# A planner's lengths of transfers, the place of one weight's sums, and the rank of early norms, in a fused attention and expert kernel

## The chip, the cores and the metric

The kernel runs on one core of one Trainium2 chip. The metric is the time of one execution in device microseconds, as the median of several runs. The core has a matrix engine (TensorE, PE in the profile), a vector engine (VectorE, DVE), a scalar engine (ScalarE, ACT), GpSimd (POOL), and SyncE (SP), which here only issues transfers. Each of them works through its own list of instructions in order.

## The reference, cut to what matters

Eight sequences of 576 tokens with 8 heads of 64 go through a linear attention without softmax, are normed, and become 4608 rows of 512. Each row goes to the one of eight experts with the largest logit, up to a capacity, in the order of the rows, and the expert is two matrix products with a Relu between them.

```python
kv = np.einsum('bhsd,bhse->bhde', k, v)
out = np.einsum('bhsd,bhde->bhse', q, kv)
rms = np.sqrt(np.mean(out * out, axis=-1, keepdims=True) + 1e-06)
x = (out / rms * g_norm) ...            # to [4608, 512]
logits = x @ w_gate
expert_idx = np.argmax(logits, axis=1)
...
h = np.maximum(np.einsum('ecd,edf->ecf', disp, w1), 0.0)
y = np.einsum('ecf,efd->ecd', h, w2)
out[i] = gate_w[i] * y[expert_idx[i], pos[i]]
```

## The kernel before, in words

**Attention, batch by batch.** For each of the eight batches (b0 to b7) `load` brings k, v and q in halves through SyncE's queue. `kv_products` multiplies k by v (L740), copies the result off the accumulators (`kvs`), turns it (L764) and forms the gate's products (L773). `unit` then makes the five blocks of the output (L801), each half copied to `o_sb` (L698 on ScalarE, L700 on VectorE), and `squares` squares them on ScalarE (L822) and sums them on VectorE (L827). `route` turns the sums into the row scale (L851, L855, L858, L865 to L870), forms the logits (`lt`, `lg`), their maximum (L899) and the one-hot choice `ohe` (L919). TensorE counts positions (the products at L944, "place" below, which wait for `ohe`), and enters the tokens into a table in PSUM (L984). The batch's rows then go to `x_dram` through GpSimd's queue (L1003, L1005).

**The early expert.** After b2 one expert is picked. Its weights come through the buffer `raw` in quarters of 512 KB each (L346): first w1, and then, through the same buffer, w2. Each weight is split into two half-precision parts. `split_weight` takes a bound on its size for each of eight pieces, either by VectorE's maximum (`top`, L362) or by ScalarE's sum of absolute values (`sum`, L366). `most` and `spread` (L370 to L377, one product on TensorE) and `scale` (L381 to L386) make a factor of it, then ScalarE writes eight upper halves (`w1h`, L391) and VectorE eight lower halves (`w1l`, L397). After b4 the table is read a first time, and the first 384 rows of the early expert are gathered (L448, GpSimd), normed (`xm`, L456, VectorE), turned (L467, TensorE), copied (the cast at L698) and split (L475). With these TensorE forms the early products: the hidden layer (L552, evicted as `hh` by ScalarE, L557, and `hl` by VectorE, L560), and the second product (L599) of three tiles.

**The rest.** When all eight batches are in the table it is read again (L1066), the experts are ranked, and round r0 gathers the early expert's other rows (L448). Rounds r1 to r7 take the other experts in order of size, each with weights and rows of its own that are prepared beside the round before. TensorE has work almost without a gap there.

**What sets the order.** Nothing runs by priority on the chip. `Plan.place` makes the lists ahead of time: each step is an `op` with a cost for each engine that may do it, the steps that it depends on, and a key. At each turn the engine that can begin first takes, of its ready steps, the one with the smallest key. A step of kind D is a transfer; its cost is how long the planner thinks it lasts. `FREE` says when each engine begins, `WKEYS` the keys of the early weights (29.5 and 38.0 with 0.3 a step), `LOW` the key of the early rows' steps (36.5), `TOPS` which engine takes the eight bounds, `WAFTER` behind which load of k, v or q a quarter of the weight may be issued.

```python
at = max(free[e], o.at[e])
...
mine.append((at, o.at[e] - o.ahead if e in FIFO else o.key, o.n, o, t))
...
loads[-1].late = 7 if r > 1 else LATE[3]
```

Of the kernel before, what the change touches and what calls it, by code (L numbers as in the profile page):

```python
# [19 lines left out]
EARLY = 384  # L20
# [13 lines left out]
ORDER = (("k", 0), ("v", 0), ("k", 1), ("v", 1), ("q", 0), ("q", 1))  # L34
FREE = {"T": 2.0, "A": 2.5, "V": 3.0, "P": 8.0, "D": 4.5, "S": 0.7}
FIFO = ("D",)
WAIT = {}
ISSUE = (0.8, 1.6)
AHEAD = 8.0
WAFTER = ((34, 36, 38, 40), (40, 40, 40, 40))  # L40
LAG = {("T", "T"): 0.0, ("A", "T"): 0.27, ("A", "V"): 0.15, ("V", "P"): 0.16, ("V", "A"): 0.15, ("A", "A"): 0.14,
# [3 lines left out]
SQUARES = 'AAAAA'  # L45
TOPS = ('VVVV', 'AAAA')
TOKENS = ('V', 0.31)
# [13 lines left out]
LOW = 36.5  # L61
LOAD = 1.46
WKEYS = ((29.5, 0.3), (38.0, 0.3))
# [98 lines left out]
def attention_moe_kernel(  # L162
# [561 lines left out]
    def kv_products(b, ts):  # L724
# [7 lines left out]
        def product(i):  # L732
            def go(e):
                a.t = a.t or bank("a")
                for c in range(C):
                    for g in range(2):
                        h = 2 * (i % 2) + g
                        k0 = c * MD + (h * D if c < C - 1 else g * D)
                        v0 = TD + k0 if c < C - 1 else (CD + h * D, g * D)[i % 2]
                        nc.tensor.matmul(a.t[rows[g], i * D:(i + 1) * D], lhsT=kh.t[:, k0:k0 + D], rhs=vh.t[:, v0:v0 + D],  # L740
                                         start=(c == 0), stop=(c == C - 1))

            kh, vh = ts["k", i // 2][0], ts["v", i // 2][0]
            return op(("T", 0.8), go, [ts["k", i // 2][1], ts["v", i // 2][1]], key, (a,), (kh, vh))

# [44 lines left out]
    def unit(b, n, ts, kv, ready, oh):  # L790
        c, key = CHUNKS[n], b * C + n
        o_sb, done = oh.t, []
        for half in range(2):
# [12 lines left out]

            o = op(("T", 0.55), product, [qd] + ready, key + half * 0.1, (ph,), (qh, kv))
            done.append(op([("A", 0.29), ("V", 0.37)], out_, [o], key + half * 0.1, (oh,), (ph,)))
# [30 lines left out]
    def route(b, oh, ssh, outs, sums):  # L839
# [106 lines left out]

        bp = op(("T", 0.7), place, [ohe] + accs[-2:-1] + reads[-1:], FIRST)

# [42 lines left out]
        o2 = V(0.4, low_hot, [lo], takes=(lh,))  # L991
        ent = op(("T", 0.21), enter, [o, o2] + enters[-1:] + readers.pop("tab", []), FIRST, (), (rh, lh))
        enters.append(ent)
# [16 lines left out]
        for first in range(2):  # L1010
            o = op(("P", 0.6), write(first), [gate, kept], key, (), (oh,))
            ws.append(op(("D", (2.05, 1.65)[first]), None, [o], key, (), (oh,)))
            ws[-1].ahead = AHEAD
# [58 lines left out]
    def early_weights():  # L1072
# [11 lines left out]
        for i, key in ((0, W1_KEY), (1, W2_KEY)):  # L1084
            loads = [op(("S", 0.43), lambda e, i=i, p=p: load_weight(i, early["reg"], raw1, p, 4),
                        [reg] + free[p], key) for p in range(4)]
            waits.append((loads, WAFTER[i]))
            loads = [op(("D", 1.46), None, [o]) for o in loads]
            for o in loads:
# [24 lines left out]
    def early_slots():  # L1114
        key = (EARLY_AFTER + 1) * C
        early["count"] = count(cnt_early, key)
        o = op(("V", 1.0), lambda e: read_table(), enters[-1:], key)
        readers.setdefault("tab", []).append(o)

        def cut(e):  # L1120
            early["gi"], early["si"] = slots(ep, first_i[0:1, 1:2])

        o = op(("V", 0.6), cut, [o] + early["picked"], key)
        early["slots"] = [o]
        x, _, _, early["turns"] = rows(lambda: (early["gi"], None), 0, EARLY, (EARLY_AFTER + 1) * S, early["slots"], key, LOW, ep,
                                       at, lambda: bank("x"))
        early["x"] = lambda: x["rows"]
# [357 lines left out]
    def weights(r, key, after):  # L1485

        ws, sets, zs, holds = wsets[r % 2], [], [], []
        for i in range(2):
# [9 lines left out]
            for p in range(4):  # L1498
# [3 lines left out]
                regs.setdefault("op", o)  # L1502
                loads.append(op(("D", 1.46), None, [o], key, (), (raws[p],)))
                loads[-1].late = 7 if r > 1 else LATE[3]
# [188 lines left out]
```

## Time and profile before

| | us |
|---|---|
| median of 3 runs | 546.19 (542.9 to 546.37) |
| the profiled execution | 548.66 |
| its span in the trace | 546.7 |
| PE busy | 505.5 (92%) |
| DVE busy | 380.1 (70%) |
| ACT busy | 239.9 (44%) |
| POOL busy | 168.5 (31%) |

The profile is of one execution. Its span is what the trace covers, and 2.0 us lie around it. Busy shares are means over the stages; the trace shows a first stage of some 120 us, in which transfers and the routing set the pace, and then 425 us in which TensorE is nearly always busy.

### The profile page before, as it was taken

What the parts mean: (1) busy time and instruction counts of PE and PEld (TensorE: products, weight loads), DVE (VectorE), ACT (ScalarE), POOL (GpSimd) and SP (SyncE); (2) the same over time, 40 slices, a digit from 0 to 9 for tenths busy, and PEclk for the clock granted to TensorE, in tenths of its full rate; (3) what the DMA queues carried; (4) which work ended last, traced back from release to release, by engine and by line L of the source; (5) the groups of instructions that cost most, each with busy time, mean ns of one, the idle gap of its engine ahead of it and who ended that gap; (6) DMA issues with size and microseconds to landing.
All of it is one profiled execution on the core that took longest, in us unless ns stands there. A gap on an engine that the chain in (4) does not pass through costs nothing.

```text
span 546.7 us, 11248 instructions
## 1 busy us (share of the span) xinstructions
PE 505.5 (92%) x4298; PEld 345.2 (63%) x4298; DVE 380.1 (70%) x1010; ACT 239.9 (44%) x462; POOL 168.5 (31%) x174
## 2 busy tenths in 40 slices
PE   4999785759989999999999999999999999999995
PEld 4898784736446666456744764776487468648743
DVE  3499878797659899999998898397667617103800
ACT  2577463885125633826624533445262544212211
POOL 2001002000242462474327323442554164021012
PEclk9899897959999999999999999999999999999999
DMA  8999999260395885792968836463755042010010
GB/s 307 419 420 418 421 424 397 81 251 1 126 359 151 199 265 172 205 331 56 207 237 217 222 115 209 124 178 113 215 155 157 33 124 43 5 60 21 2 40 31
DMA packets 62955, 102.65 MB, mean 188 GB/s; under 512 B 38636, under 2 KB 38636, under 8 KB 61874
## 3 DMA queue, kind: packets, MB, share of 16 engines
q1 hardware_dynamic: 55296, 70.50, 40.6%
q0 software_dynamic: 7584, 31.38, 16.6%
q8 instruction: 35, 0.57, 0.4%
q14 instruction: 22, 0.18, 0.1%
q10 hardware_dynamic: 18, 0.02, 0.0%
HBM read 73.20 MB, written 20.68 MB: 172 GB/s over the span
## 4 chain that ended last, share of the span: by engine, by line
issue 32%; DVE 25%; PE 21%; POOL 13%; DMA 5%; ACT 3%; POOLq 0%; DVEq 0%; SPq 0%; ACTq 0%
DVE am L362 5%; PE yp L599 5%; POOL out_dram L629 4%; PE hp L552 4%; PE op L801 4%; PE op L552 3%; POOL pair L485 3%; DVE w1l L397 3%; POOL xm L456 3%; DVE ss L827 3%; POOL xg L448 2%; DMA xs<-pair 2%; DVE w2l L397 2%; PE a L740 2%; DVE hl L560 1%
## 5 line engine op out<-in xcount | busy, mean ns | idle before, releaser
L552 PE MATMUL hp<-xs,w1h 128*128 128x320 f16 (+6 forms) x960 | 133.9, 292 | 3.3 <-DVE hl L560 2.0
L552 PEld LDWEIGHTS <-w1h 128*128 128x128 f16 x1024 | 100.1, 98 | 39.0 <-issue 7.2
L599 PEld LDWEIGHTS <-hh 128*128 128x128 f16 x560 | 54.4, 98 | 64.2 <-issue 1.3
L629 POOL DMA_INDIRECT out_dram<-ysb,si x42 | 45.2, 1075 | 161.0 <-ACT ysb L624 154.9
L557 ACT ACTIVATE hh<-hp 128x320 f16<-128x320 f32 (+7 forms) x64 | 40.9, 639 | 101.6 <-PE hp L552 101.6
L362 DVE TENSOR_REDUCE am<-raw 128x1 f32<-128x512 f32 x120 | 75.8, 674 | 3.5 <-DMA raw<-in_moe_w_dram 3.5
L552 PE MATMUL hp<-xs,w1l 128*128 128x320 f16 (+6 forms) x480 | 72.0, 292 | 0.0
L560 DVE SCALAR_TENSOR_TENSOR hl<-hp,hh 128x320 f16<-128x320 f32 (+7 forms) x64 | 47.4, 741 | 30.2 <-ACT hh L557 29.8
L624 ACT ACTIVATE ysb<-yp,ysc 128x512 f32<-128x512 f32 (+5 forms) x41 | 28.0, 684 | 90.1 <-PE yp L599 82.7
L599 PE MATMUL yp<-w2h,hh 128*128 128x512 f16 x272 | 64.4, 379 | 0.8 <-ACT ysb L624 0.8
L599 PE MATMUL yp<-w2l,hh 128*128 128x512 f16 x272 | 64.6, 379 | 0.0
L599 PE MATMUL yp<-w2h,hl 128*128 128x512 f16 x272 | 64.3, 379 | 0.0
L552 PEld LDWEIGHTS <-w1l 128*128 128x128 f16 x512 | 50.2, 98 | 16.9 <-issue 0.5
L801 PE MATMUL op<-kv_bd,in_sb 128*128 128x144 f32 x320 | 52.3, 317 | 6.6 <-ACT o_sb L698 5.0
L397 DVE SCALAR_TENSOR_TENSOR w2l<-raw,sw,w2h 128x512 f16<-128x512 f32 x64 | 55.1, 901 | 1.8 <-ACT w2h L391 1.8
L448 POOL DMA_INDIRECT xg<-x_dram,gi x42 | 43.1, 1025 | 33.6 <-DVE gt L461 12.5
L485 POOL TENSOR_TENSOR pair<-xm,pair 128x512 f16<-128x512 f32 (+5 forms) x30 | 35.9, 1198 | 55.8 <-ACT pair L481 55.6
L801 PEld LDWEIGHTS op<-kv_bd,in_sb 128*128 128x128 f32 x320 | 46.6, 212 | 8.4 <-ACT o_sb L698 5.2
L614 DVE COPY yt<-yp 128x256 f32<-128x256 f32 (+4 forms) x7 | 2.9, 411 | 70.0 <-PE yp L608 60.8
L397 DVE SCALAR_TENSOR_TENSOR w1l<-raw,sg,w1h 128x512 f16<-128x512 f32 x64 | 50.9, 846 | 0.1
L599 PEld LDWEIGHTS <-hl 128*128 128x128 f16 x280 | 27.3, 98 | 32.5
L391 ACT ACTIVATE w2h<-raw,sw 128x512 f16<-128x512 f32 x64 | 41.5, 712 | 9.4 <-PE yp L608 7.2
(227 smaller groups left out, 574.6 us busy)
## 6 DMA issues: line engine op xcount, KB each, us to landing
raw<-in_moe_w_dram SPq DMA_DIRECT2D x64, 512.0 KB, 5.2
in_sb<-in_k_dram SPq DMA_DIRECT2D x16, 576.0 KB, 8.5
v_sb<-in_v_dram SPq DMA_DIRECT2D x32, 288.0 KB, 8.6
in_sb<-in_q_dram SPq DMA_DIRECT2D x16, 576.0 KB, 11.0
x_dram<-o_sb POOLq DMA_DIRECT2D x8, 720.0 KB, 5.4
x_dram<-o_sb POOLq DMA_DIRECT2D x8, 576.0 KB, 8.8
xg<-x_dram,gi POOLq DMA_INDIRECT x42, 4.5
out_dram<-ysb,si POOLq DMA_INDIRECT x42, 3.3
```

What stands on the lines that cost most here:

```text
L362: nc.vector.tensor_reduce(out=am()[:, p:p + 1], in_=raw[:, sl(p)], axis=AX.X, op=ALU.max, apply_absolute_value=True)
L391: nc.scalar.activation(wh[:, sl(p)], raw[:, sl(p)], AF.Copy, scale=z["s"])
L397: nc.vector.scalar_tensor_tensor(out=wl[:, sl(p)], in0=raw[:, sl(p)], scalar=z["s"], in1=wh[:, sl(p)], op0=ALU.mult, op1=ALU.subtract)
L448: nc.gpsimd.indirect_dma_start(out=self.xg[i][0:n], out_offset=None, in_=x_dram[0:self.rows, :], in_offset=bass.IndirectOffsetOnAxis(ap=se ...
L485: eng.tensor_tensor(out=pair[0:n, 1], in0=self.xm[i][0:n], in1=pair[0:n, 0], op=ALU.subtract)
L552: nc.tensor.matmul(self.view(hp)[:, v], lhsT=w[:, c, f * P:(f + 1) * P], rhs=x[:, c, u * hw:(u + 1) * hw], start=(t == 0 and c == 0), stop ...
L557: nc.scalar.activation(self.out(self.hh, j), self.view(hp), AF.Relu)
L560: nc.vector.scalar_tensor_tensor(out=self.out(self.hl, j), in0=self.view(hp), scalar=0.0, in1=self.out(self.hh, j), op0=ALU.max, op1=ALU.s ...
L599: nc.tensor.matmul(yp[0:n, 0:DM], lhsT=h[:, j, o:o + n], rhs=w[:, j, :], start=(m == 0), stop=(m == len(self.terms) - 1))
L624: nc.scalar.activation(self.ysb[0:n], yp[0:n, 0:DM], AF.Copy, scale=self.ysc[0:n, i:i + 1])
L629: nc.gpsimd.indirect_dma_start(out=(disjoint.pop() if disjoint else out)[:, :], out_offset=bass.IndirectOffsetOnAxis(ap=self.sidx[0:n, col ...
L801: nc.tensor.matmul(ph.t[:, i * 2 * XW:(i + 1) * 2 * XW], lhsT=qh.t[:, q0:q0 + P], rhs=kv.t[:, 2 * half + i].rearrange("p g x -> p (g x)"), ...
```

## The change

The planner's costs are given new values: a quarter of a weight lasts 1.27 in place of 1.46, a half of k, v or q 1.41 in place of 1.46, a batch's two writes 1.76 and 1.41 in place of 2.05 and 1.65, TensorE's products of k and v 0.68 in place of 0.8, those of the output 0.49 in place of 0.55, the place products 0.3 in place of 0.7 and the table's 0.6 in place of 0.21. The queue's start is 3.3 in place of 4.5. All four quarters of the early w1 may be issued behind the same load. The eight bounds of the early w1 become ScalarE's sums. The early rows' norms and what follows them get key 32.0 in place of 36.5.

```diff
-FREE = {"T": 2.0, "A": 2.5, "V": 3.0, "P": 8.0, "D": 4.5, "S": 0.7}
+FREE = {"T": 2.0, "A": 2.5, "V": 3.0, "P": 8.0, "D": 3.3, "S": 0.7}
...
-WAFTER = ((34, 36, 38, 40), (40, 40, 40, 40))
+WAFTER = ((34, 34, 34, 34), (40, 40, 40, 40))
...
-TOPS = ('VVVV', 'AAAA')
+TOPS = ('AAAA', 'AAAA')
...
-LOAD = 1.46
+NORM = 32.0
+LOAD = 1.41
+QUARTER = 1.27
...
-            loads = [op(("D", 1.46), None, [o]) for o in loads]
+            loads = [op(("D", QUARTER), None, [o]) for o in loads]
...
-            return op(("T", 0.8), go, [ts["k", i // 2][1], ts["v", i // 2][1]], key, (a,), (kh, vh))
+            return op(("T", 0.68), go, [ts["k", i // 2][1], ts["v", i // 2][1]], key, (a,), (kh, vh))
...
-            ws.append(op(("D", (2.05, 1.65)[first]), None, [o], key, (), (oh,)))
+            ws.append(op(("D", (1.76, 1.41)[first]), None, [o], key, (), (oh,)))
...
-        x, _, _, early["turns"] = rows(lambda: (early["gi"], None), 0, EARLY, (EARLY_AFTER + 1) * S, early["slots"], key, LOW, ep,
+        x, _, _, early["turns"] = rows(lambda: (early["gi"], None), 0, EARLY, (EARLY_AFTER + 1) * S, early["slots"], key, NORM, ep,
```

All lists change order, since a cost moves every choice behind it. Two added lines at the top move the line numbers of the new kernel by 2. Three places show what stands where.

First, ScalarE and TensorE at the end of b5 (`o_sb_223` is b5's output, `sq` its squares, `am` the bounds of w1). ScalarE before:

```order
L822 ACTIVATE sq<-o_sb_223 128x512
L855 ACTIVATE lnv<-vh 128x40
L858 ACTIVATE yi<-lnv 128x40
L698 COPY o_sb_223<-nry 128x40
L928 ACTIVATE ex<-dl 128x40
L698 COPY kvs<-a 128x256
```

ScalarE now:

```order
L824 ACTIVATE sq<-o_sb_223 128x512 x2
L368 ACTIVATE w1l_177,am_1353<-raw_175 128x512 x5
L857 ACTIVATE lnv<-vh 128x40
L368 ACTIVATE w1l_177,am_1353<-raw_175 128x512
L860 ACTIVATE yi<-lnv 128x40
L700 COPY o_sb_223<-nry 128x40
L393 ACTIVATE w1h_176<-raw_175,sg 128x512 x3
L930 ACTIVATE ex<-dl 128x40
```

TensorE there before, from the last output of b5 to the place products of b5:

```order
L801 MATMUL op<-kv_bd_163,in_sb_80 128x144 x2
L740 MATMUL a<-v_sb_83,in_sb_77 64x64 x20
L740 MATMUL a<-v_sb_84,in_sb_78 64x64 x20
L944 LDWEIGHTS ones_119
L944 MATMUL misc<-ohe,ones_119 128x40
```

TensorE now:

```order
L742 MATMUL a<-v_sb_83,in_sb_77 64x64 x20
L379 LDWEIGHTS ones_b
L379 MATMUL misc<-diag,ones_b 128x128
L742 MATMUL a<-v_sb_84,in_sb_78 64x64 x20
L766 MATMUL a<-ident,kvs 128x128 x2
L803 MATMUL op<-kv_bd_162,in_sb_75 128x144 x4
L775 MATMUL a<-wgs,kvt 128x32 x2
L946 LDWEIGHTS ones_119
L946 MATMUL misc<-ohe,ones_119 128x40
```

Two sums stand ahead of b5's last squares, six stand between the squares and b5's root, and the upper halves of w1 follow at once; the product that spreads the bound stands ahead of the last product of k and v, and b5's place products stand behind b6's first outputs.

Second, VectorE where the early rows' first norm (`xm`) stands. Before:

```order
L397 SCALAR_TENSOR_TENSOR w1l_177<-raw_175,sg,w1h_176 128x512
L867 TENSOR_TENSOR nrt<-nrt,yi 128x40
L397 SCALAR_TENSOR_TENSOR w1l_177<-raw_175,sg,w1h_176 128x512
L870 SCALAR_TENSOR_TENSOR nry<-nrt,yi 128x40
L827 TENSOR_REDUCE ss_222<-sq 128x8
L882 TENSOR_TENSOR lt<-o_sb_219,nry 128x320
L456 TENSOR_TENSOR xm<-xg 128x512
```

Now:

```order
L979 TENSOR_TENSOR rhs<-ohh,tok_hl 128x480
L829 TENSOR_REDUCE ss_220<-sq 128x8 x2
L399 SCALAR_TENSOR_TENSOR w1l_177<-raw_175,sg,w1h_176 128x512
L829 TENSOR_REDUCE ss_220<-sq 128x8 x2
L399 SCALAR_TENSOR_TENSOR w1l_177<-raw_175,sg,w1h_176 128x512
L829 TENSOR_REDUCE ss_220<-sq 128x8
L829 TENSOR_REDUCE ss_222<-sq 128x8
L458 TENSOR_TENSOR xm<-xg 128x512
```

The first norm still stands right behind the last lower half of w1, but now the lower halves lie between b5's routing and b6's sums (`ss_220`), and b6's root comes behind the norm. From the first lower half to the first norm VectorE's list holds 8 lower halves, 6 sums of squares, 5 copies off the accumulators, 12 short steps of b5's routing and its 3 one-hot steps.

Third, VectorE at the end of the early hidden layer, where b7's choice `ohe` stands (`o_sb_221` is b7). Before:

```order
L912 SCALAR_TENSOR_TENSOR oh<-dl,desc 128x40
L996 TENSOR_REDUCE o_sb_221<-ex 128x5
L397 SCALAR_TENSOR_TENSOR w2l_179<-raw_175,sw_1848,w2h_178 128x512
L560 SCALAR_TENSOR_TENSOR hl<-op,hh 128x384
L916 TENSOR_REDUCE mv_all<-oh 128x5
L919 SCALAR_TENSOR_TENSOR ohe<-oh,mv_all 128x40
L925 TENSOR_REDUCE ohe<-ohe 128x8
L560 SCALAR_TENSOR_TENSOR hl<-op,hh 128x384
L950 TENSOR_TENSOR inc<-misc,ohe 128x40
```

Now:

```order
L399 SCALAR_TENSOR_TENSOR w2l_179<-raw_175,sw_1868,w2h_178 128x512
L562 SCALAR_TENSOR_TENSOR hl<-op,hh 128x384
L914 SCALAR_TENSOR_TENSOR oh<-dl,desc 128x40
L998 TENSOR_REDUCE o_sb_221<-ex 128x5
L918 TENSOR_REDUCE mv_all<-oh 128x5
L921 SCALAR_TENSOR_TENSOR ohe<-oh,mv_all 128x40
L927 TENSOR_REDUCE ohe<-ohe 128x8
L952 TENSOR_TENSOR inc<-misc,ohe 128x40
```

The eighth and last `hl` stood behind b7's choice and now stands ahead of it.

## Rows read from the trace of the kernel before

**Rows 1.** Windows of 10 us: busy us of each engine, granted clock, DMA share, GB/s.

```profile
90.00:100.00 10.00, 7.68 (x52) 7.28 (x52) 5.45 (x24) 4.40 (x13) 4.42 (x5) 0.60 0.86 321
100.00:110.00 10.00, 6.40 (x52) 6.16 (x51) 9.64 (x24) 9.88 (x24) 0.00 (x0) 1.00 0.01 3
110.00:120.00 10.00, 4.28 (x19) 3.12 (x20) 9.50 (x29) 9.23 (x27) 1.16 (x2) 0.59 0.66 229
160.00:170.00 10.00, 9.42 (x68) 6.58 (x69) 9.28 (x30) 2.36 (x6) 1.91 (x2) 1.00 0.75 296
```

**Rows 2.** SyncE's queue from 62 us; transfers of the raw weight, 60 to 140.

```profile
64.63 1.43 SPq L346 DMA_DIRECT2D raw<-in_moe_w_dram  x3
...
79.30 0.34 SPq L346 DMA_DIRECT2D raw<-in_moe_w_dram  x1
...
raw<-in_moe_w_dram SPq DMA_DIRECT2D x8, 512.0 KB, 8.3
```

**Rows 3.** ScalarE in order of time: start us, us, what.

```profile
83.73 0.63 ACT L822 ACTIVATE sq<-o_sb 128x512 f32<-128x512 f32 x1
...
102.46 0.70 ACT L698 COPY o_sb<-op 128x288 f32<-128x288 f32 x2
...
105.23 3.83 ACT L391 ACTIVATE w1h<-raw,sg 128x512 f16<-128x512 f32 x6
...
114.67 0.59 ACT L698 CAST xs<-x 128x512 f16<-128x512 f32 x1 [0.35 <-PE x L467]
...
115.78 0.62 ACT L366 ACTIVATE w2l<-raw 128x512 f16<-128x512 f32 x1
```

**Rows 4.** VectorE in order of time, 60 to 130.

```profile
85.99 1.27 DVE L362 TENSOR_REDUCE am<-raw 128x1 f32<-128x512 f32 x2
...
99.37 1.28 DVE L827 TENSOR_REDUCE ss<-sq 128x8 f32<-128x512 f32 x2
...
102.34 0.15 DVE L370 TENSOR_REDUCE a<-am 128x1 f32<-128x8 f32 x1
...
106.06 2.08 DVE L397 SCALAR_TENSOR_TENSOR w1l<-raw,sg,w1h 128x512 f16<-128x512 f32 x3
...
112.77 0.69 DVE L456 TENSOR_TENSOR xm<-xg 128x512 f32<-128x512 f32 x1
```

**Rows 5.** TensorE in order of time, the idle time before and its releaser in brackets.

```profile
91.85 0.30 PE L944 MATMUL misc<-ohe,tri 128*128 128x8 f16 x5 [3.44 <-DVE ohe L919]
...
94.11 4.62 PE L801 MATMUL op<-kv_bd,in_sb 128*128 128x144 f32 x20
...
99.13 4.16 PE L801 MATMUL op<-kv_bd,in_sb 128*128 128x144 f32 x32
...
103.19 3.21 PE L801 MATMUL op<-kv_bd,in_sb 128*128 128x144 f32 x24
111.39 1.07 PE L801 MATMUL op<-kv_bd,in_sb 128*128 128x144 f32 x4 [4.99 <-ACT o_sb L698]
...
120.75 4.00 PE L552 MATMUL op<-xs,w1h 128*128 128x384 f16 x12 [0.41 <-ACT xs L698]
```

**Rows 6.** TensorE from the end of the early hidden layer to round r0.

```profile
140.11 0.18 PE L944 MATMUL misc<-ohe,ones 128*128 128x40 f16 x1
...
155.30 1.89 PE L599 MATMUL yp<-w2h,hl 128*128 128x512 f16 x8
...
161.03 1.90 PE L552 MATMUL hp<-xs,w1h 128*128 128x320 f16 x12 [0.46 <-ACT xs L698]
```

**Rows 7.** VectorE at the end of the routing.

```profile
139.97 0.56 DVE L560 SCALAR_TENSOR_TENSOR hl<-op,hh 128x384 f16<-128x384 f32 x1 [0.63 <-ACT hh L557]
...
144.63 0.27 DVE L1066 SCALAR_TENSOR_TENSOR tab_sb<-slot_pos,cap,tab 128x48 f32<-128x48 f32 x1 [1.91 <-PE tab L984]
```

**Rows 8.** GpSimd's queue after the second table.

```profile
146.47 1.03 POOL L629 DMA_INDIRECT out_dram<-ysb,si  x1 [7.48 <-ACT ysb L624]
147.81 1.01 POOL L448 DMA_INDIRECT xg<-x_dram,gi  x1 [0.31 <-DVE cmp L1055]
```

More of the change, by code (lines that the diff above doesn't have):

```diff
@@ L805, in out_ @@
                 copy(e, o_sb[:, c, half * HH:(half + 1) * HH].rearrange("p h x -> p (h x)"), ph.t[:, 0:4 * XW])
-            o = op(("T", 0.55), product, [qd] + ready, key + half * 0.1, (ph,), (qh, kv))
+            o = op(("T", 0.49), product, [qd] + ready, key + half * 0.1, (ph,), (qh, kv))
             done.append(op([("A", 0.29), ("V", 0.37)], out_, [o], key + half * 0.1, (oh,), (ph,)))
@@ L945, in place @@
                                  stop=(i == len(terms) - 1), skip_group_check=True)
-        bp = op(("T", 0.7), place, [ohe] + accs[-2:-1] + reads[-1:], FIRST)
+        bp = op(("T", 0.3), place, [ohe] + accs[-2:-1] + reads[-1:], FIRST)
         def mine():
@@ L991, in route @@
         o2 = V(0.4, low_hot, [lo], takes=(lh,))
-        ent = op(("T", 0.21), enter, [o, o2] + enters[-1:] + readers.pop("tab", []), FIRST, (), (rh, lh))
+        ent = op(("T", 0.6), enter, [o, o2] + enters[-1:] + readers.pop("tab", []), FIRST, (), (rh, lh))
         enters.append(ent)
@@ L1502, in weights @@
                 regs.setdefault("op", o)
-                loads.append(op(("D", 1.46), None, [o], key, (), (raws[p],)))
+                loads.append(op(("D", QUARTER), None, [o], key, (), (raws[p],)))
                 loads[-1].late = 7 if r > 1 else LATE[3]
```

## Prediction

> **What bounds the kernel now.** I read the windows first [rows 1], then TensorE's timeline and what ended its gaps [rows 5], then VectorE's and ScalarE's rows behind those gaps [rows 3, 4]. From the first early product at 120.75 [rows 5] TensorE has work almost without a gap, so the time is that start, plus TensorE's work, plus one more gap before round r0. Ahead of 120.75 TensorE is not the bound: it is busy 4.28 of 10 us from 110 to 120, while VectorE has 9.50 and ScalarE 9.23 [rows 1]. The gaps have three reasons. The place products of b5 wait 3.44 us for its choice [rows 5], which VectorE makes late because it takes w1's maxima between the steps of that route [rows 4]. The last outputs of b7 wait 4.99 us for a copy [rows 5], since ScalarE writes w1's upper halves first [rows 3]. And the first norm is at 112.77, behind the last lower half [rows 4]. The second bound is the table: it is read at 144.63 [rows 7], the gathers follow at 147.81 [rows 8], and r0 begins at 161.03, 16.4 us behind the table [rows 6]. TensorE's early products end shortly after 157 (the last eight begin at 155.30 and last 1.89), so it has idled about 3 us there. A gain ahead of 120.75 counts only as far as the table comes earlier too.
>
> **The change part by part, and its sum.**
>
> *The fourth quarter.* Three quarters are issued at 64.63 and the fourth at 79.30; transfers of these land in 8.3 us at the median [rows 2]. Issued together, all four are there before 79. Its room in the queue, about 1.3 us, is taken from b7's k and v, for whose last product TensorE has to wait for the spread of the bound anyway (below). I cost that at nothing; if the cover is gone it is 1.3 us.
>
> *The sums.* ScalarE's sums follow each other at 0.61 us (0.62 a piece, the short read of the result beside it) [rows 3]; VectorE's maxima take 0.60 (two in 1.27 with the overlap of the records) [rows 4]. So eight sums are 4.9 us, put on ScalarE, and 4.8 us leave VectorE. A sum that wasn't overlapped by its read could cost 0.8: that bound adds 1.2 us for the six that count.
>
> The Trainium skill speaks against this move: "ScalarE: Activation LUTs", section "Rules for kernel authors", gives max and its like to VectorE, and estimates about 0.3 us for an instruction and 0.83 ns an element, which for 512 elements makes 0.73 us by that page. By the page the six sums would come 0.7 us later than by the row; the trace has the same instruction on w2, so the row decides, and in this shape it shows no advantage of VectorE.
>
> *When w1 is ready.* b5's last square begins at 83.73 before [rows 3]; with two sums ahead of it it ends near 85.3. Five sums (3.05), b5's logarithm (0.25) and the sixth (0.6) end at 89.2. From the bound's first step at 102.34 to the first upper half at 105.23 it took 2.9 us [rows 3, 4], and b5's route now mixes four steps in but one sum of squares goes: the upper halves begin at 92.1, 13.1 us earlier. That is not the gain, because VectorE's list puts the lower halves between the steps of b5's route and ahead of b6's sums.
>
> *The first norm.* The first lower half followed the first upper one by 0.83 us [rows 3, 4], so it starts at 92.9. From it to the norm stand 8 lower halves at 0.66 (5.3), 6 sums of squares at 0.60 (3.6), 5 copies at some 0.37 (1.9; ScalarE's take 0.35 [rows 3], and two engines differ little in this), 12 short steps at 0.1 (1.3) and three one-hot steps (1.1): 13.2 us, and 0.9 for waits on b5's place products, which now come at about 98 in place of 91.85 [rows 5]. The norm is at 107.0, 5.8 us earlier than 112.77. ScalarE must agree: its upper halves end near 99.2, then it has 16 copies (5.7) and 8 squares at 0.55 (4.4) before the cast of the first rows, which is at 109.3 against 114.67, 5.4 earlier. From the norm to the first early product it was 8.0 us (112.77 to 120.75) and the chain is the same: **the early products begin near 115.0, 5.7 us earlier.**
>
> *TensorE in between.* b6 and b7 are 80 records of output products (20, 32, 24 and 4) [rows 5]. Eight now stand ahead of b5's place products and 72 behind. At 0.13 us each (32 in 4.16) they need 9.4 us, at 0.23 (20 in 4.62) 16.6; the longer ones are in the window with a granted clock of 0.60, which is a mix of the 1.2 and the 2.4 GHz level [rows 1, 5]. I take the shorter ones behind a first two us, 10.5 us, so TensorE ends its outputs at 108.5 and the first norm is turned in time.
>
> *The table.* From the first early product to b7's place products it was 19.4 us (120.75 to 140.11 [rows 6]). Now the eighth `hl` stands ahead of b7's choice, and that one began at 139.97 behind a wait for the last product [rows 7]; it lasts 0.5 and four short steps follow, so place comes 20.5 us behind the start. From place to the table it was 4.5 us with an `hl` in it; without that, but with twelve products ahead of the table's, about 4.1. So the table is read near 139.6, 5.0 us earlier. From table to r0 I keep 16.4. It may get shorter: the first gather stood behind a write to the output that was issued at 146.47 because its tile was late [rows 8]; that tile now comes a little earlier relative to the table, which frees up to 1.3 us. **r0 begins 5.0 to 6.3 us earlier; I take 5.3,** near the lower end, because three gathers and the weights of r1 still share the transfers.
>
> *What follows.* r1's weights and rows are prepared on VectorE beside r0, where it is 9.28 of 10 us busy [rows 1], and they hang on the rank, which moves with the table. The new order there moves a norm to GpSimd and w1's bound behind one more `hl`; TensorE's list also takes one more group of upper-half products before the first lower ones. I cost this at nothing; without that cover it is up to 2 us. The other new lengths of transfers change only orders that I count through these lists.
>
> The sum: span 546.7 less 5.3 is 541.4, the profiled time 543.4, and since the median of the runs (546.19) lies 2.5 below the profiled execution, 540.9; I give **541.0**.
>
> **The rivals.**
>
> *The gain is larger.* If the gathers land as soon as TensorE is done, r0 follows the early products directly: their 36.4 us from 120.75 to 157.2, behind 115.0, end at 151.4, and with the turns of the last rows 152.5, 8.5 us earlier: 537.7. For it: gathers leave ahead of r1's weights. Against it: the table is worked out above at 139.6, and 16.4 us behind it is 156.
>
> *It is given back in r1.* If VectorE's order beside r0 makes w1's lower halves 2 to 4 us late, TensorE waits at r1 and the net gain is 1 to 3: 544.5. For it: VectorE is nearly full there [rows 1]. Against it: its total work there falls by one norm.
>
> *TensorE stays at the low clock, and the kernel is slower.* TensorE's list holds the spread of w1's bound ahead of the last product of k and v. That spread waits for ScalarE's eighth sum until some 89, so TensorE idles about 5 us just ahead of the outputs, and again for b5's choice. If all 72 records run at 0.23 they end at 114.6, turns and casts then take the 7.2 us that they took before, the early products begin at 121.8, and with the 1.1 us that b7's choice loses the time is 548. It decides from about 60 slow records of the 72 on. For it: 0.60 granted in the very window that follows the wait of 3.44, and 0.59 behind that of 4.99 [rows 1, 5]. Against it: there the stretch of long records ended within 20 records. "TensorE: Matmul & The Clock Gate" of the Trainium skill, section "HAM oscillation — how this bites in real kernels", says that gaps put the array back on its lower clock and that each burst behind one starts at it; by that rule the price is paid at each of these gaps, and the trace agrees with it in both places.
>
> **How the numbers follow.** A measurement of this kernel tells about 1% (5.5 us) from no change. The forecast (539.5 to 543) has 0.43, the larger gain 0.17, given back (543 to 546.5) 0.26, slower 0.14. The range 536 to 549 leaves out a tenth at each end at most: below it the larger gain with a faster r1, above it the low clock with a loss in r1. Faster by over 1% is below 540.7: the larger gain and just under half of the forecast, 0.37. Slower by over 1% is above 551.7, half of the third case with r1 late: 0.07. Within 1%: 0.56.
>
> **What would show it.** In the changed kernel's trace: four quarters issued within 2 us near 65; the first upper half of w1 near 92; b5's place products near 98 with a wait of some us ahead; the first norm near 107, the first early product near 115, the table near 139.6, r0 near 155.7, and an idle TensorE of some 4 us just before r0. The forecast is wrong if the norm comes early but the products at 120 (clock or ScalarE's copies), if the table doesn't follow the products, or if r1 shows waits that were not there.

## The result and the profile after

The changed kernel took 540.82 us (median of 12, 538.32 to 543.89) against 548.33 for the kernel before in the same jobs (median of 12): ratio 0.9886, 95% interval 0.9858 to 0.9915. It is faster by about 1.1%. The ratios here and below leave out some slow executions, nearly all of them of the kernel before, so they are not the quotients of the medians. The profiled execution took 542.44 with a span of 540.3, 6.4 less than before.

The first view is the windows of 10 us of the changed kernel, with the columns of [rows 1].

```profile
90.00:100.00 10.00, 8.27 (x70) 8.09 (x67) 8.07 (x30) 7.41 (x17) 4.02 (x5) 0.55 0.67 248
100.00:110.00 10.00, 8.17 (x71) 7.71 (x69) 9.83 (x25) 9.97 (x27) 0.00 (x0) 1.00 0.81 278
110.00:120.00 10.00, 7.31 (x37) 4.11 (x38) 7.98 (x32) 7.26 (x23) 1.16 (x2) 0.66 0.32 133
```

TensorE is busy 7.31 of 10 us from 110 to 120 where it was 4.28, since the early products have begun. The two windows with a low granted clock are still there, 0.55 and 0.66 [rows 1].

ScalarE and VectorE of the changed kernel in order of time, one fence each, answer to [rows 3] and [rows 4, 7].

```profile
83.17 1.13 ACT L824 ACTIVATE sq<-o_sb 128x512 f32<-128x512 f32 x2
84.21 0.62 ACT L368 ACTIVATE w1l<-raw 128x512 f16<-128x512 f32 x1
...
87.40 0.61 ACT L368 ACTIVATE w1l<-raw 128x512 f16<-128x512 f32 x1
...
91.10 1.95 ACT L393 ACTIVATE w1h<-raw,sg 128x512 f16<-128x512 f32 x3 [0.89 <-DVE sg L388]
...
108.52 0.70 ACT L700 CAST xs<-x 128x512 f16<-128x512 f32 x1
```

```profile
88.14 0.16 DVE L372 TENSOR_REDUCE a<-am 128x1 f32<-128x8 f32 x1 [1.69 <-ACT w1l L368]
...
91.95 0.74 DVE L399 SCALAR_TENSOR_TENSOR w1l<-raw,sg,w1h 128x512 f16<-128x512 f32 x1
...
106.92 0.68 DVE L458 TENSOR_TENSOR xm<-xg 128x512 f32<-128x512 f32 x1
...
134.08 0.55 DVE L562 SCALAR_TENSOR_TENSOR hl<-op,hh 128x384 f16<-128x384 f32 x1
...
139.54 0.26 DVE L1068 SCALAR_TENSOR_TENSOR tab_sb<-slot_pos,cap,tab 128x48 f32<-128x48 f32 x1 [1.04 <-PE tab L986]
...
173.38 0.15 DVE L463 TENSOR_SCALAR gt<-xg 128x1 f32<-128x1 f32 x1 [2.38 <-DMA xg<-x_dram,gi]
173.46 1.86 DVE L364 TENSOR_REDUCE am<-raw 128x1 f32<-128x512 f32 x3
```

w1's bound is taken at 88.14 where it was 102.34, the first norm is at 106.92 where it was 112.77, and the table is read at 139.54 where it was 144.63. The last two rows are new: beside r0 VectorE waits 2.38 us for a gather of r1's rows, and three maxima of r1's w2 stand behind that wait.

TensorE of the changed kernel answers to [rows 5, 6].

```profile
85.40 2.40 PE L742 MATMUL a<-v_sb,in_sb 128*64 128x64 f32 x40 [2.11 <-DMA v_sb<-in_v_dram]
88.87 0.27 PE L379 MATMUL misc<-diag,ones_b 128*128 128x128 bf16 x1 [1.07 <-DVE diag L376]
...
93.20 0.69 PE L766 MATMUL a<-ident,kvs 128*128 128x128 f32 x2 [1.73 <-DVE kvs L702]
93.68 2.12 PE L803 MATMUL op<-kv_bd,in_sb 128*128 128x144 f32 x8
...
96.31 0.22 PE L946 MATMUL misc<-ohe,ones 128*128 128x40 f16 x1
...
96.61 9.27 PE L803 MATMUL op<-kv_bd,in_sb 128*128 128x144 f32 x64
...
114.40 2.08 PE L554 MATMUL op<-xs,w1h 128*128 128x384 f16 x6 [0.67 <-ACT xs L700]
...
152.53 1.79 PE L554 MATMUL hp<-xs,w1h 128*128 128x320 f16 x12 [0.65 <-ACT xs L700]
...
176.36 0.22 PE L379 MATMUL pt_max<-diag,ones_b 128*128 128x128 bf16 x1 [1.61 <-DVE diag L376]
...
181.60 0.19 PE L610 MATMUL yp<-hh,w2l 128*128 128x64 f16 x1 [0.48 <-issue]
181.63 0.59 PE L554 MATMUL hp<-xs,w1h 128*128 128x336 f16 x3
```

The waits of 3.44 for b5's choice and 4.99 for b7's copy are gone, and in their place are 1.07 and 1.73 ahead of the outputs of b6 and b7, which begin at 93.68. The early products begin 6.35 us earlier. Round r0 (152.53) begins 8.5 us earlier than 161.03. Of that, 2.1 are lost by the start of r1, which came at 188.00 before and comes at 181.63, 6.4 earlier. Two stops that the kernel before doesn't have make them up: 1.61 at 176.36, the spread of r1's w2, and 0.48 just ahead of r1, for which the trace names no cause. From r1 to the end of the span it is 358.7 us in both kernels, so all of the difference lies ahead of r1.

Last, the queues behind the table in the changed kernel: GpSimd's first write and first gather, and SyncE's first transfers of r1's weights (these began at 149.18 before).

```profile
139.93 1.03 POOL L631 DMA_INDIRECT out_dram<-ysb,si  x1 [3.71 <-ACT ysb L626]
141.98 1.00 POOL L450 DMA_INDIRECT xg<-x_dram,gi  x1 [1.02 <-DVE cmp L1052]
...
144.69 5.80 SPq L348 DMA_DIRECT2D raw<-in_moe_w_dram  x8
```

The first gather leaves 2.4 us behind the table, not 3.2, and leads the weights by 2.7 us, not 1.4 [rows 8]. The write still stands ahead of it in GpSimd's list, but it leaves at 139.93 and no longer holds it up.

### The profile page after: what moved, and what is told of

Read it like the earlier page. It is cut to its first block, busy times and chain, and to the rows that moved or that the text cites. A ratio compares the mean times of both kernels' runs of the same rounds, so it can differ in the third digit from the quotient of the medians.

```text
span 540.3 us, 11261 instructions
## 1 busy us (share of the span) xinstructions
PE 506.4 (94%) x4298; PEld 347.4 (64%) x4298; DVE 375.2 (69%) x1003; ACT 243.4 (45%) x478; POOL 167.9 (31%) x173
## 4 chain that ended last, share of the span: by engine, by line
PE 35%; issue 31%; POOL 12%; DVE 12%; ACT 5%; DMA 2%; POOLq 1%; DVEq 0%; ACTq 0%; SPq 0%
PE yp L601 11%; PE hp L554 10%; POOL out_dram L631 4%; PE op L803 4%; PE op L554 3%; POOL pair L487 3%; POOL xm L458 3%; PE a L742 2%; DVE am L364 2%; POOL xg L450 2%; DVE ss L829 2%; ACT sq L824 1%; DMA xg<-x_dram,gi 1%; DVE hl L562 1%; DMA v_sb<-in_v_dram 1%
## 5 line engine op out<-in xcount | busy, mean ns | idle before, releaser
L631 POOL DMA_INDIRECT out_dram<-ysb,si x42 | 46.9, 1116 | 162.8 <-ACT ysb L626 157.5
L364 DVE TENSOR_REDUCE am<-raw 128x1 f32<-128x512 f32 x112 | 70.6, 675 | 4.0 <-DMA raw<-in_moe_w_dram 3.3
L626 ACT ACTIVATE ysb<-yp,ysc 128x512 f32<-128x512 f32 (+5 forms) x41 | 28.1, 685 | 92.1 <-PE yp L601 75.2
L399 DVE SCALAR_TENSOR_TENSOR w1l<-raw,sg,w1h 128x512 f16<-128x512 f32 x64 | 52.1, 858 | 0.0
L487 POOL TENSOR_TENSOR pair<-xm,pair 128x512 f16<-128x512 f32 (+5 forms) x27 | 32.2, 1191 | 42.7 <-ACT pair L483 42.5
```

Of the source, the lines that this page charges most:

```text
L364: nc.vector.tensor_reduce(out=am()[:, p:p + 1], in_=raw[:, sl(p)], axis=AX.X, op=ALU.max, apply_absolute_value=True)
L399: nc.vector.scalar_tensor_tensor(out=wl[:, sl(p)], in0=raw[:, sl(p)], scalar=z["s"], in1=wh[:, sl(p)], op0=ALU.mult, op1=ALU.subtract)
L487: eng.tensor_tensor(out=pair[0:n, 1], in0=self.xm[i][0:n], in1=pair[0:n, 0], op=ALU.subtract)
L626: nc.scalar.activation(self.ysb[0:n], yp[0:n, 0:DM], AF.Copy, scale=self.ysc[0:n, i:i + 1])
L631: nc.gpsimd.indirect_dma_start(out=(disjoint.pop() if disjoint else out)[:, :], out_offset=bass.IndirectOffsetOnAxis(ap=self.sidx[0:n, col ...
```

## The experiments

### Undoing one part of the change

Each of the first four is the changed kernel with one part undone.

```diff
-TOPS = ('AAAA', 'AAAA')
+TOPS = ('VVVV', 'AAAA')
```

> The changed kernel with the eight bounds of the early w1 taken by VectorE's maxima again; the quarters behind one load, the rank and the lengths stay. Theory one (the start of the early products sets the gain, and the sums on ScalarE are a part of it because VectorE is full from 100 to 120 us): 4.8 us of maxima come back into VectorE's list ahead of the first norm, of which half displaces lower halves that now stand behind the norm; the first early product comes near 117 in place of 114.4 and the time is 543 to 544 in place of 540.8. Rival (VectorE has that room, since it waits for b5's place products anyway): the products begin within 0.7 us of 114.4 and the time is 540 to 541.5.

Measured: 542.66 us, ratio to before 0.9879 (0.9818 to 0.9941). The maxima move w1's bound from 88.14 to 92.64, but the first norm comes at 106.90 as with the sums, because three of the eight lower halves then fall behind it, and the products begin at 114.94. The rival holds for the start: the products come within 0.6 us, which single traces can't tell from nothing (last section). The median lies between the two theories, and the ratio is that of the changed kernel (0.9886) within the intervals, so the time decides nothing.

```diff
-NORM = 32.0
+NORM = 36.5
```

> The changed kernel with the early rows' key at 36.5 again, nothing else. Theory one (the quarters and the sums bring w1's bound forward, and the norm merely follows the last lower half): the first norm stands one row later in VectorE's list, the first early product comes within 1 us of 114.4 and the time is 540 to 542. Rival (the rank is what brings the norm forward, as it did in the sum's step of the first norm): the norm falls back towards 112.8, the products to 118 or later, and the time to 544 or more.

Measured: 543.10 us, 0.9876 (0.9804 to 0.9947). The first norm is at 107.28 and the products begin at 115.58, 1.2 us later, which is theory one's bound to 0.2 and far from the rival's 118: the rank does little there. The median is a microsecond above theory one's, while the ratio (0.9876) can't be told from the changed kernel's. In the trace r0 comes 17.2 us behind the table (155.78), where the changed kernel needs 13.0, but r1 then starts only 1.3 us later than there.

```diff
-WAFTER = ((34, 34, 34, 34), (40, 40, 40, 40))
+WAFTER = ((34, 36, 38, 40), (40, 40, 40, 40))
```

> The changed kernel with the quarters of w1 behind four different loads again. Theory one (without the fourth quarter by 79 us the sums can't end early, so the bound falls back and with it the upper and lower halves): the bound's first step comes near 99 to 102 in place of 88.1, the first early product 4 to 6 us later, near 119 to 120, and the time is 544 to 546. Rival (ScalarE's upper halves are quick enough, and the norm now stands ahead of the lower halves): the products begin near 115 to 116 and the time is 541 to 542.

Measured: 545.66 us, 0.9962 (0.9921 to 1.0002). The bound falls back to 101.50, as theory one said, and yet the products begin at 113.79, because the planner puts the norm ahead of seven lower halves; so theory one fails on the products and the rival on the time. The time is lost behind the table: it is read at 139.87, as in the changed kernel, but r0 needs 16.25 us from there.

```diff
-FREE = {"T": 2.0, "A": 2.5, "V": 3.0, "P": 8.0, "D": 3.3, "S": 0.7}
+FREE = {"T": 2.0, "A": 2.5, "V": 3.0, "P": 8.0, "D": 4.5, "S": 0.7}
...
-LOAD = 1.41
-QUARTER = 1.27
+LOAD = 1.46
+QUARTER = 1.46
...
```

> The changed kernel with all the old costs (4.5, 1.46, 1.46, 0.8, 0.55, 0.7, 0.21, 2.05 and 1.65), so that only the quarters, the sums and the rank are changed against the kernel before. Theory one (the three edits carry the gain, and the lengths only reorder): the bound is taken near 88 to 91, the first early product begins within 1.5 us of 114.4, and the time is 540 to 542.5. Rival (the lengths decide where b5's place products, b7's choice and the gathers stand): the first early product near 114 to 116 but the table or round r0 2 to 4 us later, and a time of 543 to 546.

Measured: 552.91 us, 1.0108 (1.0065 to 1.0151): the three edits without the lengths are slower than the kernel before. Theory one falls, and so does the rival, which also had the products near 114 to 116. TensorE in order of time shows where the start is lost:

```profile
86.11 1.39 PE L742 MATMUL a<-v_sb,in_sb 128*64 128x64 f32 x40
93.19 0.27 PE L379 MATMUL misc<-diag,ones_b 128*128 128x128 bf16 x1 [5.69 <-DVE diag L376]
94.20 0.19 PE L946 MATMUL misc<-ohe,ones 128*128 128x40 f16 x1 [0.74 <-DVE bmax L383]
...
94.55 2.40 PE L742 MATMUL a<-v_sb,in_sb 128*64 128x64 f32 x40
99.51 0.69 PE L766 MATMUL a<-ident,kvs 128*128 128x128 f32 x2 [2.56 <-issue]
...
101.56 2.27 PE L803 MATMUL op<-kv_bd,in_sb 128*128 128x144 f32 x8
...
120.93 1.44 PE L554 MATMUL op<-xs,w1h 128*128 128x384 f16 x4 [0.67 <-ACT xs L700]
```

The spread of w1's bound and b5's place products both stand ahead of the last 40 products of k and v. TensorE waits 5.69 us for the bound with those products queued behind it, and the outputs begin at 101.56 in place of 93.68. The lower halves are done near 105.7, but the squares and copies of the late outputs stand ahead of the norm (113.53). That takes back what the three edits won at the start, and no more: r0 begins at 160.96, as in the kernel before (161.03). The loss against that kernel lies behind it, since from r0 to r1 it is 32.1 us in place of 27.0. TensorE stops there for 0.87, 0.27 and 0.90 us behind VectorE and ScalarE, and for 2.0 in five stops for which the trace names no cause (last section); no run tried these.

### The lengths alone, and the one place that they decide

The kernel before with the costs of the diff alone:

```diff
-LOAD = 1.46
+LOAD = 1.41
+QUARTER = 1.27
...
```

> The kernel before with the new lengths and costs alone; the quarters, the maxima and the rank stay as before. Theory one (the lengths carry a large part, since the three edits with the old costs came out at 552.9): b7's products of k and v run without a stop, b5's place products follow them, the first early product comes 2 to 4 us earlier than 120.75, near 117 to 118, and the time is 543 to 545.5. Rival (neither half gains alone): the first early product within 1 us of 120.75 and the time 547 to 549.

Measured: 547.80 us, 1.0031 (0.9994 to 1.0068). The rival holds for the time, and not for the start of the products, which came later, at 122.34: TensorE is through with b7's outputs by 107.5, but w1's maxima are late (bound at 103.64), so it idles 7.51 us for the norm. So neither half gains alone, and both together do. The next run asks whether it is that one place in TensorE's list: it has the old costs, and only two steps planned later.

```diff
         accs.append(V(0.11, number, [ohe] + accs[-1:]))
+        ohe.late = 4.0 if b == 5 else 0.0
...
             o = op(("V", 0.5), lambda e, f=f: f["most"](), tops, key)
+            o.late = 6.0 if i == 0 else 0.0
```

> The three edits with the old costs, as in the run of 552.9, but b5's choice planned 4 us and w1's bound 6 us later, so that TensorE's list holds b7's last products of k and v ahead of b5's place products and of the spread of w1's bound. Theory one (with the old costs these two stand ahead of those products, TensorE idles 5.7 us there, and b7's outputs, the squares and the norm all follow late): the stop of 5.7 us goes, the outputs begin near 93 to 95 in place of 101.6, the first early product near 115 to 117 in place of 120.9, and the time is 545 to 548, since the long way from table to r0 stays. Rival (the norm is late for VectorE's own list): the first early product stays at 119.5 or later and the time at 550 or more.

Measured: 542.10 us, 0.9862 (0.9783 to 0.9942), 10.8 us less than without these two lines (by the medians, and by the spans too: 551.0 and 540.2). TensorE now:

```profile
88.01 2.16 PE L742 MATMUL a<-v_sb,in_sb 128*64 128x64 f32 x40 [2.78 <-DMA v_sb<-in_v_dram]
91.57 0.69 PE L766 MATMUL a<-ident,kvs 128*128 128x128 f32 x2 [1.39 <-ACT kvs L700]
...
93.59 0.29 PE L379 MATMUL misc<-diag,ones_b 128*128 128x128 bf16 x1
93.68 7.03 PE L803 MATMUL op<-kv_bd,in_sb 128*128 128x144 f32 x36
...
114.78 1.62 PE L554 MATMUL op<-xs,w1h 128*128 128x384 f16 x7 [1.01 <-ACT sq L824]
```

Theory one holds for the start: the spread waits for nothing, the outputs begin at 93.68 and the products at 114.78. The time is better than it said, because r0 also comes 13.1 us behind the table, where it had kept the long way. Of the 10.8 us the start has 6.2; at r0 it is 8.4, and at r1 11.4, and what lies behind the start came with other moves of the lists that no run took apart. The new lengths are not needed for the gain: an order that doesn't hold b7's products behind w1's bound did as well without them.

### From the table to r0

Two runs moved the gathers against r1's weights. The first was meant to put the first early write behind them:

```diff
+            if r < 0 and i == 0:
+                o.late = 5.0
```

> The kernel before with the first early write to the output planned 5 us later, so that it stands behind round r0's three gathers in GpSimd's queue instead of ahead of them. Theory one (16.4 us from table to r0 become 13.0 where the gathers leave ahead of r1's weights, which in the kernel before start at 149.18, beside the second gather): the gathers leave 1.3 us earlier, the second and third land 3 us or more earlier, TensorE goes from its early products to r0 with less than 1.5 us of idle time, r0 begins at 158 to 159 in place of 161.0, and the time is 545.5 to 547. Rival (only the place in the queue counts): r0 begins at most 1.3 us earlier, 159.7 or later, with gathers that last as long as before, and the time is within 1 us of the kernel before.

Measured: 548.16 us, 1.0037 (0.9980 to 1.0094). The write still went ahead of the gathers (its list ends before theirs begins), so this tells nothing of the theories; the edit moved only later steps. The same move, made by planning the write in the second list:

```diff
+            if r < 0 and i == 0:
+                early["write"] = go, o, yh
+                continue
...
+    go, o, yh = early["write"]
+    o = op(("P", 1.1), go, [o, sent[-1]], -KEY, (), (yh,))
```

> The kernel before with the first early write to the output moved behind round r0's three gathers on GpSimd (the edit before this left it ahead of them). Theory one (from table to r0 it takes 13 us where the first gather leaves 2 to 2.7 us ahead of r1's weights, and 15.7 to 18.7 where it leads by 1.4 or less): the first gather leaves about 2 us behind the table in place of 3.2, r0 begins 13.5 to 14.5 us behind the table in place of 16.4, and the time is 545 to 547.5 against about 548 for the kernel before. Rival (only the place in the queue counts): r0 begins 15.2 or more behind the table and the time doesn't change by 1 us.

Measured: 547.64 us, 1.0042 (0.9989 to 1.0095). The first gather leaves 2.5 us behind the table and leads the weights by 2.04; r0 follows at 14.6 (145.18 to 159.77) in place of 16.4. That is theory one's place to 0.1 us. The time shows no gain, as the rival had it: r1 begins at 188.44, 28.7 us behind r0 in place of 27.0. Three stops of TensorE without a cause in the trace, 1.4 us in all, are the most of that (last section); whether they come of the edit isn't shown.

The other way round, in the changed kernel a transfer of two rows stands ahead of the gathers:

```diff
+                if raw is None:
+                    pad = pool.tile([P, XR], F32, name="pad", bufs=1)
+                    nc.gpsimd.indirect_dma_start(
+                        out=pad[0:2], out_offset=None, in_=x_dram[0:n, :],
+                        in_offset=bass.IndirectOffsetOnAxis(ap=st["rows"].gidx[0:2, 3:4], axis=0))
```

> The changed kernel with one more indirect transfer of two rows ahead of round r0's gathers, so that these leave 1.3 us later against r1's weights, as they did before; all lists are else the same. Theory one (the order of gathers and weights on the transfers decides): the second gather leaves beside the first weight quarter and lands some 7 us behind its issue in place of 5, r0 begins at 155.5 to 156.5 in place of 152.5, that is 16 us behind the table, and the time is 542.5 to 544.5. Rival (only the place in the queue counts): r0 begins at 152.9 to 153.8 and the time is 540.8 to 542.

Measured: 543.34 us, 0.9948 (0.9907 to 0.9989). GpSimd's, SyncE's and VectorE's rows of it:

```profile
141.33 0.95 POOL L1142 DMA_INDIRECT pad<-x_dram,gi  x1 [1.16 <-DVE rank L1054]
142.58 0.98 POOL L450 DMA_INDIRECT xg<-x_dram,gi  x1 [0.30 <-issue]
...
143.99 6.17 SPq L348 DMA_DIRECT2D raw<-in_moe_w_dram  x8
...
147.70 0.69 DVE L458 TENSOR_TENSOR xm<-xg 128x512 f32<-128x512 f32 x1 [4.56 <-DMA xg<-x_dram,gi]
```

Here r0 is at 154.41, 15.7 us behind a table read at 138.74. Counted from the table the gathers left 1.4 us later and r0 came 2.7 later, so half is the place in the queue, and for the other half the transfers took longer: the first gather takes 5.1 us to its norm (142.58 to 147.70) where it took 3.9 (141.98 to 145.84), and VectorE waits 7.0 us for the three gathers in all, where it waited 2.0.

But the lead alone doesn't set how long the first gather takes. In the kernel before, with the same lead of 1.4, it took 3.6 us (147.81 to 151.37), and it was the second and the third that came late. VectorE there, and in the changed kernel, where only the first is waited for:

```profile
151.37 0.69 DVE L456 TENSOR_TENSOR xm<-xg 128x512 f32<-128x512 f32 x1 [0.97 <-DMA xg<-x_dram,gi]
...
156.41 0.15 DVE L461 TENSOR_SCALAR gt<-xg 128x1 f32<-128x1 f32 x1 [4.28 <-DMA xg<-x_dram,gi]
...
157.51 0.15 DVE L461 TENSOR_SCALAR gt<-xg 64x1 f32<-64x1 f32 x1 [0.94 <-DMA xg<-x_dram,gi]
```

```profile
145.84 0.69 DVE L458 TENSOR_TENSOR xm<-xg 128x512 f32<-128x512 f32 x1 [1.99 <-DMA xg<-x_dram,gi]
```

The times of all runs, in us, by how far the first gather leads the weights; "waits" is what VectorE waits for r0's gathers in all:

| run | lead | waits | table to r0 | first product | r0 | r1 | r1 to end |
|---|---|---|---|---|---|---|---|
| a_oldlen | -0.1 | 8.5 | 18.7 | 120.93 | 160.96 | 193.06 | 357.9 |
| a_lowrank | 0.7 | 6.1 | 17.2 | 115.58 | 155.78 | 182.89 | 357.8 |
| before | 1.4 | 6.2 | 16.4 | 120.75 | 161.03 | 188.00 | 358.7 |
| b_behind | 1.4 | 4.0 | 15.7 | 119.21 | 158.63 | 185.44 | 360.1 |
| a_delay | 1.4 | 7.0 | 15.7 | 114.73 | 154.41 | 183.53 | 358.7 |
| a_apart | 1.4 | 6.4 | 16.3 | 113.79 | 156.12 | 185.36 | 357.7 |
| b_lengths | 2.0 | 2.1 | 13.0 | 122.34 | 159.85 | 188.73 | 358.0 |
| b_write | 2.0 | 5.2 | 14.6 | 121.27 | 159.77 | 188.44 | 357.7 |
| a_later | 2.0 | 2.0 | 13.2 | 113.28 | 149.89 | 179.70 | 360.7 |
| after | 2.7 | 2.0 | 13.0 | 114.40 | 152.53 | 181.63 | 358.7 |
| a_maxima | 2.7 | 1.9 | 13.0 | 114.94 | 153.03 | 182.32 | 358.0 |
| a_gates | 2.7 | 5.3 | 14.1 | 113.52 | 152.32 | 180.36 | 359.4 |
| o_behind | 2.7 | 2.1 | 13.1 | 114.78 | 152.59 | 181.69 | 358.5 |

With a lead of 2.0 us or more r0 follows the table within 13.0 to 14.6, with 1.4 or less it takes 15.7 to 18.7. The waits sort the runs more finely: 1.9 to 2.1 go with 13.0 to 13.2, and 5.2 and 5.3 with 14.6 and 14.1. a_gates, which has the changed kernel's lists up to r0 and its lead, is one of the latter, so the lead isn't the whole, and a column of one trace each is good to 1 us only. Where the waits are 2 us TensorE's own early products fill the time up to r0, but for the stops in it (0.84 us in the changed kernel), so faster gathers would win little more.

### What is given back in r0

```diff
-            o.late = 9 if r > 1 else 1.2
+            o.late = 9 if r > 1 else 3.6
```

> The changed kernel with the gathers of r1's rows planned 3.6 us late in place of 1.2, so that VectorE takes r1's maxima ahead of the steps that wait for a gather. Theory one (TensorE's new wait of 1.6 us at the spread of r1's w2 comes from VectorE's 2.4 us behind a gather, with three maxima behind that): both waits go, r1 begins 1.5 to 2 us earlier against r0, and the time is 538.5 to 539.5. Rival (r1 is then held by another step, its rows or the lower halves): the wait moves into r1 and the time is 540.3 to 541.5.

Measured: 540.06 us, 0.9916 (0.9873 to 0.9959). TensorE at the spread of r1's w2 and later:

```profile
173.51 0.22 PE L379 MATMUL pt_max<-diag,ones_b 128*128 128x128 bf16 x1
...
178.98 0.26 PE L610 MATMUL yp<-hh,w2l 128*128 128x64 f16 x3 [0.44 <-issue]
```

The wait of 1.61 is gone, so its cause is settled: VectorE's wait for a gather ahead of the maxima. From r0 to r1 it is 28.0 us in place of 29.1 (27.0 before): the last 1.1 are stops of TensorE of 0.44, 0.42 and 0.20 without a cause in the trace (last section). 0.7 comes back behind r1; theory one's time is missed by half a microsecond. The medians of the two kernels, 540.06 and 540.82, can't be told apart.

The last run goes for the start once more, on top of that edit:

```diff
+        ohe.late = 3.0 if b == 5 else 0.0
...
+            o.late = 4.0 if i == 0 else 0.0
```

> The changed kernel with r1's gathers planned later, and besides with w1's bound planned 4 us and b5's choice 3 us later, so that TensorE has all of b7's products of k and v ahead of the spread and b6's first outputs ahead of the place products. Theory one (TensorE's stops at the spread, 1.1 to 4.5 us in the runs so far, hold up b7's outputs): the outputs begin at 92 or earlier, the first early product at 112.5 to 113.5, and the time is 537.5 to 539.5. Rival (VectorE and ScalarE are full from 100 to 110 and set the norm whatever TensorE does): the norm stays near 107, the first early product near 114.4, and the time is 539.5 to 541.5.

Measured: 542.07 us, 0.9868 (0.9794 to 0.9942). The products begin at 113.28 and the table is read at 136.70, 2.8 us earlier than in the changed kernel, though the outputs begin at 93.5, not at 92: theory one is half right. Nothing is left of it at the end: r0 is 2.6 earlier, r1 1.9, and the end 0.1 later. Between r0 and r1 four stops of the same kind take 2.1 us, and from r1 to the end it is 360.7 us, the longest of the 13 traces (357.7 to 360.7); why isn't known. No version was found that beats the changed kernel by more than the measurements tell.

## Why the prediction was right, and where not

**The time** (541.0 forecast, 540.82 measured) was right, but two of its terms were off in opposite ways and nearly cancel, so that it came this close is in part luck. Besides, the offset of 2.5 us from the profiled execution to the median was read from three runs; over 12 the kernel before has its median at 548.33, 0.3 below its profile, and the kernel after 1.6 below. In spans, which the sum is about, 541.4 was forecast and 540.3 came.

**The quarters.** Four are issued from 64.15 within 3.1 us, and the first product isn't later for it: undone, it moves by 0.6 us the other way, which one trace can't tell from nothing. Costed at nothing: right.

**The sums** follow each other at 0.61 us and end at 88.0 (89.2 forecast). The first upper half is at 91.10 (92.1), the first lower half at 91.95 (92.9), the norm at 106.92 (107.0), the cast at 108.52 (109.3). From lower half to norm it took 15.0 where the sum had 14.1, so a microsecond won ahead was lost there. That the sums are a part of the gain, as the text let it stand, the runs don't show: the products start within 0.6 us without them. The same goes for the quarters and the rank: with any one of the three undone the products begin between 113.79 and 115.58, and with all three undone at 122.34. Which of them are enough together no run tells.

**The early products** begin at 114.40 (115.0). b5's place products come at 96.31 (98) and wait for nothing; the stop forecast ahead of them lies at the spread and at `kvs`, 2.8 us in all with 2.1 for v ahead of it. The 72 output records end at 107.5 (108.5).

**The low clock.** TensorE of the changed kernel in windows of 1 us: its busy time and instructions, granted clock, DMA share, GB/s.

```profile
84.00:85.00 1.00, 0.00 (x0) 1.00 1.05 429
...
86.00:87.00 1.00, 1.00 (x24) 0.50 1.03 424
...
98.00:99.00 1.00, 1.00 (x6) 0.50 1.11 309
...
100.00:101.00 1.00, 1.00 (x11) 1.00 0.91 346
```

The clock is at its lower level (0.50) when the products of k and v follow the wait of 2.11 for v, ahead of both stops, and at the upper one again from 100 on, after five microseconds of outputs. The first eight output records take 0.27 us each, the next 64 take 0.145 on average, and some 10 of the 72 that the prediction counts ran as long as 0.23, so the price never came near the 60 from which that rival decides. The rule quoted with it from "TensorE: Matmul & The Clock Gate" of the Trainium skill, section "HAM oscillation — how this bites in real kernels", agrees with the place of the fall, behind the wait for v; the stop of 1.77 us ahead of 110.09 shows no such fall, with a granted clock of 1.00 from 110 to 111. But the mechanism of that rival, the spread ahead of the last products of k and v, is what takes back the gain at the start with the old costs; it costs through what is queued behind it, outputs that begin 8 us later, and not through the clock.

**The table** is read at 139.54 (139.6). b7's place products come 21.5 us behind the start (20.5 forecast) and the table 3.65 behind them (4.1).

**From table to r0** is the first term that was mis-sized: 16.4 kept, less at most 1.3; 13.0 measured. The prediction had one reason, the write that no longer holds the gathers up, but took the place in the queue for the whole price. Its own caution, that gathers and r1's weights share the transfers, works the other way: VectorE waits 2.0 us for the three gathers in place of 6.2, and a_delay, where nothing but the gathers' place is changed, has 7.0 and an r0 that comes 2.7 later behind the table. So the rival of the larger gain came true at r0, with its 8.5 us, and TensorE idles under 1 us ahead of r0, not 4.

**What follows** is the second: nothing taken, up to 2 kept as a bound; 2.1 measured. That is the rival "given back in r1", in another place than it named: not the lower halves but the maxima, behind a wait for a gather (1.61), and a stop of 0.48 whose cause is open. With the wait gone (a_gates) only 1.1 of the 2.1 come back, since there are more such stops.

**The new lengths** were said to change only orders that the lists count. That is what they do, but the prediction didn't ask what the other edits would be without them. The runs say: the lengths alone change nothing that is measured (1.0031), the edits alone are 1.1% slower, and both together 1.1% faster.

## What to carry to other kernels

Where a planner sets the order, an edit has no price of its own: look in each engine's list for the instruction that waits, and cost what is queued behind it, since two lines that moved two such steps brought the start 6.2 us forward here, and the end 10.8. Where a short transfer that the next stage waits for runs beside bulk loads, look at which leaves first: the two edits that moved little else than that order made 1.8 (b_write, not far above what equal lists differ by) and 2.7 us (a_delay) from the table to r0. And count a gain where the execution ends and not where it is won: the 2.6 us won at r0 in the last run came to nothing by the end.

## What the runs showed of the hardware that wasn't expected

Three kernels with the same lists up to the table (after, a_delay, a_gates) begin the early products at 114.40, 114.73 and 113.52, and three others (before, b_behind, b_write) at 120.75, 119.21 and 121.27. So one trace fixes that start to 1 or 2 us only, and differences of less between traces are not read here.

In seven of the kernels TensorE stops inside r0's last small products (L610, 96 of them, 0.03 us apart) for 0.26 to 0.70 us at a time, 0.5 to 2.1 us in all, and waits for nothing that the trace shows; all 96 records are there in a_gates, where it stops twice. The kernel before has no such stop. From r0 to r1 they are what a_gates still loses against the kernel before, and the most of what b_write loses. What they are stays open: no run tried it.
